# Seven half-size products for the gate and value matrices of the last layer

## The chip, the cores and the metric
One core of one Trainium2 chip runs the whole program as one launch. The metric is the device time of an execution in microseconds (us); the kernel before has a median of 1442.25 us over three runs (1439.95 to 1443.89). Engines: TensorE (PE, its weight loads PEld), VectorE (DVE), ScalarE (ACT), GpSimd (POOL) and SyncE (SP), which issues the transfers.

## The reference
Three layers follow each other. The last one is what the change touches:

```python
def reference(**kwargs):
    attn_out = _attn_ref(**attn_kwargs)             # B=2, H=8, S=768, D=64
    x = attn_out.transpose(0, 2, 1, 3).reshape(B * S, H * D)      # 1536 x 512
    x = _moe_ref(x=x, **moe_kwargs)                 # 8 experts, 512 -> 1024 -> 512, every token in each
    return _moe2_ref(x=x, **moe2_kwargs)

def _moe2_ref(x, w_gate, w_val, w_out):             # 512 -> 1536 -> 512
    gate = 1.0 / (1.0 + np.exp(-(x @ w_gate)))
    val = x @ w_val
    return (gate * val @ w_out).astype(np.float32)
```

## The kernel before
Every large matrix product is made of three matmuls: each operand is split into a rounded part (`h`, made on ACT) and a remainder (`l`, made on POOL or DVE as the difference), and h*h, h*l and l*h are added up in PSUM (`product`, L365 to L373). Tokens stand transposed in SBUF as `xh`, `xl` (features on partitions, 4 blocks of 128 features by 1536 tokens), the result of a layer as `acc` (12 tiles of 128 tokens by 512).

The feed-forward layers run in visits. A visit takes 256 hidden features. Experts 1 to 7 have 28 visits of the kind "fast". Each goes through the two batches of 768 tokens one after the other (`pair`), and treats the product of a 512x256 weight block with 768 tokens as a 2x2 product of operand blocks: seven products of blocks with half the features, half the hidden columns and 384 tokens, in place of eight. The seven left operands are sums and differences of weight blocks (`sum_steps` on POOL, then `form_step`, which splits each on ACT and POOL), the seven right operands are token blocks or sums of token blocks (`th`, `tl`, and the block (0,1) of `xh`, `xl`, which is overwritten by a sum). Results are added across four PSUM accumulators: `copied` keeps a partial sum in SBUF (ACT), `summed` adds one back (DVE), `hidden` rounds the hidden block (ACT) and appends its remainder to the list `late` (DVE). A product whose accumulator already holds a partial sum may start only when `copied` or `summed` has read it. PSUM banks: two for x, one each for y and z, and a ring of four (Y).

Between the products stand the second products (`unit_second`): for 128 tokens, six matmuls of 512 columns with the hidden blocks of the half visited before, then one DVE accumulation into `acc`. `slots` is called after each product and each second product; there the next visit's sums and forms and other side work are issued. What is written first in the program is issued first on its engine; the schedule is this order alone (`manual_schedule`), and every engine works through its queue in order.

After the last expert visit (`last`, which issues no forms of a next visit) the kernel before changes buffers (`moe.close()`) and works in a plain form. `turn_y` (L1312 to L1324) transposes one block of 128 features of four token tiles on TensorE, copies it to `xh` on ACT and subtracts it to `xl` on DVE; four of these stand between the last six second products, eight in the first visit after. Each of the six "glu" visits (`unit_first`, kind glu) goes through three chunks of 512 tokens; for each of its two hidden blocks it makes the gate product (12 matmuls of 512 columns), a sigmoid on ACT, the value product, the product with the gate on DVE, its rounding on ACT and remainder on DVE; then come four second products of the chunk before. The weights of the six visits are read as pieces of 512 KB (gate, value, out) from a DRAM copy made earlier (`load_piece`) and split whole (`split_steps`).

Of the kernel before, what the change touches and what calls it, by code (L numbers as in the profile page):

```python
# [26 lines left out]
PACE = (8, 13)  # L27
# [39 lines left out]
def tile_global_local_attention__then__sinkhorn_moe__then__glu(  # L67
# [96 lines left out]
    for f in range(NFF):  # L164
        visits.append(dict(kind="glu", f=f, chunks=chunks, slot=1 - len(visits) % 2, load=True))
# [3 lines left out]
    G0 = len(visits) - NFF  # L169
    last = G0 - 1  # L170
    turns = []


# [37 lines left out]

    def second_steps(n):

        vis = visits[n]
        r = raw[vis["raw"]][:, 4 * FQ : 8 * FQ]
        yield from split_halves(r, wh[vis["slot"]][1], wl[vis["slot"]][1])

    def split_steps(n):

        vis, steps = visits[n], []  # L220
        for j, part in enumerate(glu_weights(vis)):
            i = 3 * vis["f"] + j
            steps += split_halves(piece(i), *part)
            steps.append(lambda i=i: load_piece(i + 4))
        return steps
# [17 lines left out]
    def glu_weights(vis):  # L243

        g, v = state["glu", vis["f"] % 2]
        return g, v, (wh[vis["slot"]][1], wl[vis["slot"]][1])

# [10 lines left out]
    def w1_blocks(n):  # L258
        r = raw[visits[n]["raw"]][:, 0 : 4 * FQ]
        r = r.rearrange("p (k f c) -> p f k c", k=KD, f=2)  # L260
        return {(i, j): r[:, i, 2 * j : 2 * j + 2, :] for i in range(2) for j in range(2)}
# [138 lines left out]
    def unit_first(n, c, tick):  # L400
        vis = visits[n]
        m = c[1] * P
        if vis["kind"] == "moe":
            at = next_hid()
            hh, hl = hid[at]
            for f in range(2):
                ps = state["A"].next()[:, :m]
                first((wh[vis["slot"]][0], wl[vis["slot"]][0]), c, f, ps)
                nc.scalar.activation(out=hh[:, f, :m], in_=ps, func=AF.Relu)
                nc.vector.scalar_tensor_tensor(  # L410
                    out=hl[:, f, :m], in0=ps, scalar=0.0, in1=hh[:, f, :m].bitcast(F32),
                    op0=ALU.max, op1=ALU.subtract,
                )
                tick()
        else:
            at = HID + state["glu_hid"]
            state["glu_hid"] = 1 - state["glu_hid"]
            hh, hl = hid[at]
            gate_w, val_w, _ = glu_weights(vis)
            for f in range(2):  # L420
                ps = state["A"].next()[:, :m]
                first(gate_w, c, f, ps)
                sg = state["sg"].next()[:, :m]
                nc.scalar.activation(out=sg, in_=ps, func=AF.Sigmoid)
                tick()
                ps = state["A"].next()[:, :m]
                first(val_w, c, f, ps)
                z = state["z"].next()[:, :m]
                nc.vector.tensor_tensor(out=z, in0=ps, in1=sg, op=ALU.mult)  # L429
                nc.scalar.activation(out=hh[:, f, :m], in_=z, func=AF.Copy)  # L430
                nc.vector.tensor_tensor(
                    out=hl[:, f, :m], in0=z, in1=hh[:, f, :m].bitcast(F32), op=ALU.subtract
                )
                tick()
        return [(n, c[0] + j, at, j) for j in range(c[1])]

    def unit_second(n, t, at, j):
# [4 lines left out]
        if vis["kind"] != "glu":  # L442
# [30 lines left out]
    def turn():  # L473
        if turns:
            turns.pop(0)[1]()

    def run_visit(n, tick, ahead, pace=None):
# [3 lines left out]
        at = 0 if visits[n]["kind"] == "moe" else 1  # L481
        per = chunks[0][1] + (4 if at else 2)
        pace = pace or PACE[at]
        ahead = Paced(ahead, per * (len(chunks) - at) * pace // 12)
        side = tick

        def tick():
            side()
            if u >= at:
                ahead.tick()  # L490

        for u, c in enumerate(chunks):
            while any(at == c for at, _ in turns):
                turn()
# [14 lines left out]
    def pair(n, b, slots):  # L509
# [3 lines left out]
        snap, pre = state["snap"], state["pre"]  # L513
        x, y, z = state["X"].next()[:, :C], state["P2"][:, :C], state["P5"][:, :C]
        t_hid, late = next_hid(), []
        pending, done = state["pending"], []

        def run(i, ps, rhs, start=True):
# [8 lines left out]
            )  # L527

# [6 lines left out]
        def rest():  # L535
            for step in late:
                step()
            late.clear()

        def seconds(count):  # L540
            for _ in range(count):
                if pending:
                    unit_second(*pending.pop(0))
                rest()
                slots(None)

        def hidden(at, f, src):
            hh, hl = hid[at]
            nc.scalar.activation(out=hh[:, f, :C], in_=src, func=AF.Relu)  # L549
            late.append(  # L550
                lambda: nc.vector.scalar_tensor_tensor(  # L551
                    out=hl[:, f, :C], in0=src, scalar=0.0, in1=hh[:, f, :C].bitcast(F32),
# [4 lines left out]
        def summed(at, f, ps, kept):  # L557
            p = pre.next()
            nc.vector.tensor_tensor(out=p, in0=ps, in1=kept, op=ALU.add)  # L559
            hidden(at, f, p)  # L560
# [6 lines left out]
        slots(0)  # L567
        run(1, z, trans(0))
        copied(1, z)
        slots(1)  # L570
# [798 lines left out]
```

## Time and profile before

| | us |
|---|---|
| median of three runs | 1442.25 |
| lowest, highest | 1439.95, 1443.89 |
| span of the profiled execution | 1437.5 |
| TensorE busy in it | 1419.4 |
| DVE, POOL, ACT busy | 864.8, 568.8, 504.7 |
| first product of the last expert visit starts at | 1091.3 |
| first product of the last layer starts at | 1132.4 |
| last matmul ends about | 1433.2 |

The profile is of one execution; the page gives its span, from the first to the last instruction, and no time beside it. Busy times are shares of that span. In a timeline each line is one instruction or several alike in a row: its start, how long it took, the engine, the source line, what it wrote and read, and in brackets how long its engine had been idle and who ended that. Matmuls overlap in the pipeline, so the distance between two starts, not the length of one, is what a matmul costs.

### The profile page before, as it was taken

The page shows a single profiled execution, that of the slowest core. Times are in us where ns is not written, and L with a number is a line of the kernel's source. Part 1 is how long each engine was busy: PE and PEld are TensorE (multiplying, and loading weights), DVE is VectorE, ACT ScalarE, POOL GpSimd, SP SyncE. Part 2 cuts the span into 40 slices and gives each one's busy share as a digit, 9 for nine tenths or more (in the row PEclk, how much of TensorE's full clock was granted, in tenths as well). Part 3 has the DMA queues.
Part 4 walks back from the last instruction along what each step waited for, and adds up shares of the span by engine and source line. Part 5 has one row for each costly group of instructions (what it writes and reads, how often), then busy time and mean ns, then how long its engine had stood idle before and what let it go on. Part 6 is the DMA issues. An engine that isn't in the chain of part 4 may idle for free.

```text
span 1437.5 us, 19809 instructions
## 1 busy us (share of the span) xinstructions
PE 1419.4 (99%) x7286; PEld 1225.3 (85%) x7287; DVE 864.8 (60%) x1655; ACT 504.7 (35%) x1152; POOL 568.8 (40%) x618
## 2 busy tenths in 40 slices
PE   8999999999999999999999999999999999999998
PEld 4666888999999999999999899999999888888887
DVE  6676476677667666767676666666665533333333
ACT  5777222433333333333333333333333322122111
POOL 4554454554345454354454444445432221112110
PEclk9999999999999999999999999999999999999999
DMA  7751011132121222221213212213210110010002
GB/s 182 162 143 46 16 45 59 45 103 73 52 74 52 73 86 69 73 74 52 74 52 103 74 55 71 73 52 103 74 38 30 44 45 15 30 44 30 0 1 88
DMA packets 99192, 92.60 MB, mean 64 GB/s; under 512 B 55312, under 2 KB 73744, under 8 KB 99088
## 3 DMA queue, kind: packets, MB, share of 16 engines
q1 hardware_dynamic: 98800, 91.26, 20.5%
q8 instruction: 59, 0.97, 0.3%
q14 instruction: 45, 0.37, 0.1%
q10 hardware_dynamic: 288, 0.00, 0.0%
HBM read 78.66 MB, written 12.58 MB: 63 GB/s over the span
## 4 chain that ended last, share of the span: by engine, by line
PE 94%; DVE 2%; ACT 1%; POOL 1%; issue 1%; DMA 0%; SPq 0%; DVEq 0%; ACTq 0%; POOLq 0%
PE bank L371 30%; PE bank L373 30%; PE bank L372 30%; PE bank L870 1%; PE bank L922 1%; PE bank L908 1%; PE bank L844 1%; ACT e L884 0%; POOL wl L205 0%; DVE e L878 0%; PE bank L1317 0%; POOL e L896 0%; DMA lens<-in_n_local_dram 0%; SPq L649 0%; DVE hl L410 0%
## 5 line engine op out<-in xcount | busy, mean ns | idle before, releaser
L454 DVE SCALAR_TENSOR_TENSOR acc<-bank,gate,acc 128x512 f32<-128x512 f32 x336 | 251.6, 749 | 226.7 <-PE bank L373 220.9
L371 PE MATMUL bank<-wh,hh 128*128 128x512 f32 x912 | 359.3, 394 | 0.0
L373 PE MATMUL bank<-wh,hl 128*128 128x512 f32 x912 | 357.6, 392 | 0.0
L205 POOL TENSOR_TENSOR wl<-raw,wh 128x512 fp32r<-128x512 f32 (+1 forms) x196 | 209.4, 1085 | 372.4 <-ACT wh L204 367.9
L372 PE MATMUL bank<-wl,hh 128*128 128x512 f32 x912 | 356.1, 390 | 0.0
L371 PE MATMUL bank<-xh,wh 128*128 128x384 f32 (+1 forms) x720 | 252.2, 350 | 1.1 <-ACT aT L909 1.1
L372 PE MATMUL bank<-xl,wh 128*128 128x384 f32 (+1 forms) x720 | 249.8, 347 | 0.0
L373 PE MATMUL bank<-xh,wl 128*128 128x384 f32 (+1 forms) x720 | 249.8, 347 | 0.0
L373 PEld LDWEIGHTS bank<-wh,hl 128*128 128x128 f32 x912 | 171.3, 188 | 37.8
L549 ACT ACTIVATE hh<-kept 128x384 fp32r<-128x384 f32 x168 | 88.2, 525 | 310.6 <-DVE kept L559 310.6
L371 PEld LDWEIGHTS bank<-wh,hh 128*128 128x128 f32 x912 | 171.5, 188 | 26.1 <-issue 1.4
L372 PEld LDWEIGHTS bank<-wl,hh 128*128 128x128 f32 x912 | 171.7, 188 | 25.1
L371 PEld LDWEIGHTS bank<-xh,wh 128*128 128x128 f32 x720 | 135.3, 188 | 15.0 <-ACT aT L909 1.3
L372 PEld LDWEIGHTS bank<-xl,wh 128*128 128x128 f32 x720 | 135.5, 188 | 13.7 <-DVE xl L1322 0.5
L373 PEld LDWEIGHTS bank<-xh,wl 128*128 128x128 f32 x720 | 135.4, 188 | 6.3
L205 POOL TENSOR_TENSOR wl<-work,wh 128x256 fp32r<-128x256 f32 x112 | 94.1, 842 | 97.7 <-ACT wh L204 97.6
L563 ACT ACTIVATE kept<-bank 128x384 f32<-128x384 f32 x168 | 82.4, 491 | 119.7 <-PE bank L373 119.5
L551 DVE SCALAR_TENSOR_TENSOR hl<-kept,hh 128x384 fp32r<-128x384 f32 x168 | 113.8, 677 | 1.4 <-ACT hh L549 1.3
L373 PE MATMUL bank<-th,wl 128*128 128x384 f32 x336 | 113.0, 336 | 0.0
L371 PE MATMUL bank<-th,wh 128*128 128x384 f32 x336 | 112.9, 336 | 0.0
L372 PE MATMUL bank<-tl,wh 128*128 128x384 f32 x336 | 112.8, 336 | 0.0
L429 DVE TENSOR_TENSOR z<-bank,sg 128x512 f32<-128x512 f32 x36 | 24.9, 692 | 138.3 <-PE bank L373 138.3
(143 smaller groups left out, 1858.2 us busy)
## 6 DMA issues: line engine op xcount, KB each, us to landing
raw<-in_moe_w_dram SPq DMA_DIRECT2D x72, 512.0 KB, 4.2
glw<-work SPq DMA_DIRECT2D x36, 256.0 KB, 2.3
raw<-glw SPq DMA_DIRECT2D x18, 512.0 KB, 3.3
work<-in_moe_w_gate_dram SPq DMA_DIRECT2D x12, 512.0 KB, 3.9
work<-in_moe_w_val_dram SPq DMA_DIRECT2D x12, 512.0 KB, 3.9
work<-in_moe_w_out_dram SPq DMA_DIRECT2D x12, 512.0 KB, 3.9
qr<-in_q_dram SPq DMA_DIRECT2D x32, 96.0 KB, 2.7
kr<-in_k_dram SPq DMA_DIRECT2D x32, 96.0 KB, 2.9
```

The costliest lines, as they stand in the source:

```text
L205: nc.gpsimd.tensor_tensor(out=lo, in0=r, in1=h.bitcast(F32), op=ALU.subtract)
L371: nc.tensor.matmul(lhsT=ah, rhs=bh, start=first, stop=False, **mm)
L372: nc.tensor.matmul(lhsT=ah, rhs=bl, start=False, stop=False, **mm)
L373: nc.tensor.matmul(lhsT=al, rhs=bh, start=False, stop=end, **mm)
L429: nc.vector.tensor_tensor(out=z, in0=ps, in1=sg, op=ALU.mult)
L454: nc.vector.scalar_tensor_tensor(out=a, in0=ps, scalar=gate[:, t, e : e + 1], in1=a, op0=ALU.mult, op1=ALU.add,)
L549: nc.scalar.activation(out=hh[:, f, :C], in_=src, func=AF.Relu)
L551: lambda: nc.vector.scalar_tensor_tensor(out=hl[:, f, :C], in0=src, scalar=0.0, in1=hh[:, f, :C].bitcast(F32), op0=ALU.max, op1=ALU.subtract,)
L563: nc.scalar.activation(out=snap[:, i], in_=ps, func=AF.Copy)
L844: nc.tensor.transpose(ps[:, j * P : (j + 1) * P], raw_[u % QKB][:, j, :], ident)
L870: nc.tensor.matmul(out=ps[j][:, lo:KW], lhsT=qT[rows, own], rhs=kT[rows, keys], start=True, stop=True,)
L908: nc.tensor.transpose(ps[:, j, a, :], e[:, j, a * P : (a + 1) * P], ident)
```

## The change
The six visits become twelve of the kind "gate" and "val" in turn, and go through `pair` and `run_fast` like the experts, in the experts' buffers (`moe.close()` and all buffers made behind it go; `sg`, room for the eight sigmoid blocks of a visit, comes in their place). A gate visit writes sigmoids only; the value visit multiplies them in. `then` places three second products in each half of a visit, after products 1, 2 and 4. The token operands are made anew by `turned`, eight steps per batch: those of batch 0 are issued after products 4, 5 and 6 of the last expert visit's second half and between its last six second products, those of batch 1 after products 1 to 6 of the first gate visit's first half (the last three steps after product 6). The last expert visit's second products of batch 0 are moved to stand after products 1, 2 and 3, two each. The results leave from `acc`.

```diff
     for f in range(NFF):
-        visits.append(dict(kind="glu", f=f, chunks=chunks, slot=1 - len(visits) % 2, load=True))
+        slot = 1 - visits[-1]["slot"]
+        visits.append(dict(kind="gate", f=f, piece=3 * f))
+        visits.append(dict(kind="val", f=f, piece=3 * f + 1, slot=slot))
...
         else:
-            o = state["o"].next()
-            nc.vector.tensor_tensor(out=o, in0=ps, in1=a, op=ALU.add)
-            nc.sync.dma_start(out=out[t * P : (t + 1) * P, :], in_=o)
+            nc.vector.tensor_tensor(out=a, in0=ps, in1=a, op=ALU.add)
+            nc.sync.dma_start(out=out[t * P : (t + 1) * P, :], in_=a)
...
+            for step in late:
+                step()
+            late.clear()
...
+        def then(i):
+            slots(i)
+            for _ in range(min(counts.get(i, 0), len(pending))):
+                unit_second(*pending.pop(0))
+                for step in late:
+                    step()
+                late.clear()
                 slots(None)
...
+            if kind == "gate":
+                nc.scalar.activation(out=state["sg"][b, half, f], in_=src, func=AF.Sigmoid)
+                return
...
+            if kind == "val":
+                z = pre.next()
+                nc.vector.tensor_tensor(out=z, in0=src, in1=state["sg"][b, half, f], op=ALU.mult)
+                nc.scalar.activation(out=hh, in_=z, func=AF.Copy)
+                late.append(
+                    lambda: nc.vector.tensor_tensor(
+                        out=hl, in0=z, in1=hh.bitcast(F32), op=ALU.subtract
+                    )
+                )
+                return
...
         def before(i):
             side()
-            if i is None and ahead:
+            if n == G0 and i is not None and i > 0:
+                trans_step(1, 3 if i == 6 else 1)
+            if ahead and (i is None or not expert):
                 ahead.pop(0)()
...
-            elif i > 0:
+                return
+            if i > 0 and more:
                 form_step(n + 1, i - 1)
+            if n == last and i > 3:
+                trans_step(0, 1)
+
+        all_ = {1: 1, 2: 1, 3: 1, 4: 1, 5: 2}
+        half = {1: 1, 2: 1, 4: 1}
+        pair(n, 0, before, all_ if expert else half)
...
+        pair(n, 1, after, {1: 2, 2: 2, 3: 2} if n == last else all_ if expert else half)
...
+                load_piece(vis["piece"] + 4)
+                if vis["kind"] == "val":
+                    load_piece(vis["piece"] + 5)
...
+        def turn(s, k, half):
+            kk = 2 * k + s
+            ps = state["Y"].next()[:, :C]
+            t0 = b * TB + half * TC
+            for j in range(TC):
+                nc.tensor.transpose(
+                    ps[:, j * P : (j + 1) * P], acc(t0 + j)[:, kk * P : (kk + 1) * P], ident
+                )
+            return ps
+
+        def whole(s, k, half, ps):
+            h, lo = tokens(k, s, b, half)
+            nc.scalar.activation(out=h, in_=ps, func=AF.Copy)
+            nc.vector.tensor_tensor(out=lo, in0=ps, in1=h.bitcast(F32), op=ALU.subtract)
+
+        def less(x, y):
+            t = temps.next()
+            nc.vector.tensor_tensor(out=t, in0=x, in1=y, op=ALU.subtract)
+            return t
+
+        def put(i, s, r):
+            th, tl = state["t"]
+            split_one(r, th[:, i, s, b, :], tl[:, i, s, b, :])
+
+        def r11(s):
+            live["r11", s] = ps = turn(s, 0, 0)
+            whole(s, 0, 0, ps)
+
+        def r12(s):
+            ps = turn(s, 0, 1)
+            live["r12", s] = r = temps.next()
+            nc.scalar.activation(out=r, in_=ps, func=AF.Copy)
+            live["t0", s] = t = less(r, live["r11", s])
+            put(0, s, t)
+
+        def r22(s):
+            ps = turn(s, 1, 1)
+            live["t1", s] = t = less(ps, live["t0", s])
+            put(1, s, t)
+            whole(s, 1, 1, ps)
+            r = live["r12", s]
+            nc.vector.tensor_tensor(out=r, in0=ps, in1=r, op=ALU.subtract)
+            put(2, s, r)
+
+        def r21(s):
+            ps = turn(s, 1, 0)
+            whole(s, 1, 0, ps)
+            split_one(less(ps, live["t1", s]), *tokens(0, s, b, 1))
+
+        return [lambda f=f, s=s: f(s) for f in (r11, r12, r22, r21) for s in range(2)]
...
+    for n in range(F0, len(visits)):
         if n == last:
             doubles.finish()
         run_fast(n, doubles.tick)
...
+        if n == last:
+            while state["pending"]:
+                unit_second(*state["pending"].pop(0))
+                trans_step(0, 1)
+            trans_step(0, 8)
     flush(no_tick)
```

## Rows read from the trace of the kernel before

**Rows 1.** The page: each engine's busy time, share of the span, instructions.
```profile
PE 1419.4 (99%) x7286; PEld 1225.3 (85%) x7287; DVE 864.8 (60%) x1655; ACT 504.7 (35%) x1152; POOL 568.8 (40%) x618
```

**Rows 2.** Windows: stretch, length, each engine's busy time and count, granted clock, DMA.
```profile
1106.83:1433.20 326.37, 326.34 (x1459) 268.82 (x1458) 119.12 (x175) 73.35 (x128) 46.37 (x36) 1.00 0.09 31
1230.00:1280.00 50.00, 50.00 (x219) 41.00 (x219) 16.82 (x25) 10.51 (x18) 7.70 (x6) 1.00 0.10 34
```

**Rows 3.** Timeline of TensorE: product 1, a unit, product 2 of the last expert visit.
```profile
1107.87 0.34 PE L371 MATMUL bank<-th,wh 128*128 128x384 f32 x1
...
1108.91 0.39 PE L371 MATMUL bank<-wh,hh 128*128 128x512 f32 x1
...
1110.28 0.34 PE L371 MATMUL bank<-th,wh 128*128 128x384 f32 x1
```

**Rows 4.** Timeline of TensorE: four transposes between second products, end of the expert layer.
```profile
1123.73 0.60 PE L1317 MATMUL bank<-ident,acc 128*128 128x128 f32 x4
1124.08 0.48 PE L371 MATMUL bank<-wh,hh 128*128 128x512 f32 x1
1124.40 0.39 PE L372 MATMUL bank<-wl,hh 128*128 128x512 f32 x1
```

**Rows 5.** Timeline of DVE in the last expert visit.
```profile
1110.48 0.75 DVE L454 SCALAR_TENSOR_TENSOR acc<-bank,gate,acc 128x512 f32<-128x512 f32 x1 [2.31 <-PE bank L373]
...
1115.98 0.55 DVE L551 SCALAR_TENSOR_TENSOR hl<-kept,hh 128x384 fp32r<-128x384 f32 x1
1116.45 0.55 DVE L559 TENSOR_TENSOR kept<-bank,kept 128x384 f32<-128x384 f32 x1
...
1118.41 1.46 DVE L551 SCALAR_TENSOR_TENSOR hl<-kept,hh 128x384 fp32r<-128x384 f32 x1
```

**Rows 6.** Timeline of ACT: last expert visit, then two operations back to back.
```profile
1108.13 0.49 ACT L563 ACTIVATE kept<-bank 128x384 f32<-128x384 f32 x1 [0.55 <-PE bank L373]
...
1114.60 0.53 ACT L549 ACTIVATE hh<-kept 128x384 fp32r<-128x384 f32 x1 [2.53 <-DVE kept L559]
...
1135.45 0.60 ACT L424 ACTIVATE sg<-bank 128x512 f32<-128x512 f32 x1 [4.99 <-PE bank L373]
1135.94 0.59 ACT L1321 ACTIVATE xh<-bank 128x512 fp32r<-128x512 f32 x1
```

**Rows 7.** Timeline of POOL beside the remainder at 1118.41.
```profile
1118.15 1.29 POOL L205 TENSOR_TENSOR wl<-raw,wh 128x512 fp32r<-128x512 f32 x1 [24.28 <-ACT wh L204]
```

**Rows 8.** Groups by line over the run: busy us, mean ns of one.
```profile
L551 DVE SCALAR_TENSOR_TENSOR hl<-kept,hh 128x384 fp32r<-128x384 f32 x168 | 113.8, 677 | 1.4 <-ACT hh L549 1.3
L205 POOL TENSOR_TENSOR wl<-work,wh 128x256 fp32r<-128x256 f32 x112 | 94.1, 842 | 97.7 <-ACT wh L204 97.6
L204 ACT ACTIVATE wh<-work 128x256 fp32r<-128x256 f32 x112 | 45.0, 404 | 0.0
L205 POOL TENSOR_TENSOR tl<-work,th 128x768 fp32r<-128x768 f32 x6 | 11.8, 1971 | 6.4 <-ACT th L204 6.4
L205 POOL TENSOR_TENSOR wgl<-raw,wgh 128x512 fp32r<-128x512 f32 x6 | 7.8, 1298 | 91.0 <-ACT wgh L204 91.0
```

**Rows 9.** Timeline of DVE and ACT: one hidden block of the first glu visit.
```profile
1138.66 0.69 DVE L429 TENSOR_TENSOR z<-bank,sg 128x512 f32<-128x512 f32 x1 [1.40 <-PE bank L373]
...
1139.39 0.63 ACT L430 ACTIVATE hh<-z 128x512 fp32r<-128x512 f32 x1 [2.85 <-DVE z L429]
...
1140.05 0.69 DVE L431 TENSOR_TENSOR hl<-z,hh 128x512 fp32r<-128x512 f32 x1 [0.70 <-ACT hh L430]
```

**Rows 10.** TensorE's clock: timeline of the start, window behind the end.
```profile
1.18 4.65 PE L693 MATMUL bank<-zeros 128*128 128x512 bf16 x12 [1.18 <-DVE zeros L689]
...
7.37 1.03 PE L693 MATMUL bank<-zeros 128*128 128x512 bf16 x4
...
1437.00:1439.00 2.00, 0.00 (x0) 0.00 (x0) 0.00 (x0) 0.00 (x0) 0.00 (x0) 0.91 0.01 4
```

**Rows 11.** DMA issues of the weight pieces: count, KB each, us to landing.
```profile
raw<-glw SPq DMA_DIRECT2D x18, 512.0 KB, 3.3
```

More of the change, by code (lines that the diff above doesn't have):

```diff
@@ L26 @@
 HID = 3
-PACE = (8, 13)
+PACE = 8
 LAG = 3
@@ L168, in tile_global_local_attention__then__sinkhorn_moe__then__glu @@
     F0 = NB0 + NQ
-    G0 = len(visits) - NFF
+    G0 = len(visits) - 2 * NFF
     last = G0 - 1
-    turns = []
     queues = [[], []]
@@ L402, in unit_first @@
         m = c[1] * P
[L403 to L434, printed above, removed]
+        at = next_hid()
+        hh, hl = hid[at]
+        for f in range(2):
+            ps = state["A"].next()[:, :m]
+            first((wh[vis["slot"]][0], wl[vis["slot"]][0]), c, f, ps)
+            nc.scalar.activation(out=hh[:, f, :m], in_=ps, func=AF.Relu)
+            nc.vector.scalar_tensor_tensor(
+                out=hl[:, f, :m], in0=ps, scalar=0.0, in1=hh[:, f, :m].bitcast(F32),
+                op0=ALU.max, op1=ALU.subtract,
+            )
+            tick()
         return [(n, c[0] + j, at, j) for j in range(c[1])]
@@ L471, in flush @@
             tick()
-    def turn():
-        if turns:
-            turns.pop(0)[1]()
     def run_visit(n, tick, ahead, pace=None):
         chunks = visits[n]["chunks"]
[L481 to L484, printed above, removed]
+        ahead = Paced(ahead, (chunks[0][1] + 2) * len(chunks) * (pace or PACE) // 12)
         side = tick
@@ L488, in tick @@
             side()
[L489 to L494, printed above, removed]
+            ahead.tick()
+        for c in chunks:
             pending = unit_first(n, c, tick)
@@ L533, in block, with hidden @@
             return lambda s: tokens(k, s, b, half)
[L535 to L544, printed above, removed]
-                slots(None)
-        def hidden(at, f, src):
-            hh, hl = hid[at]
-            nc.scalar.activation(out=hh[:, f, :C], in_=src, func=AF.Relu)
+        def then(i):
[5 more added lines that the diff above has]
+                late.clear()
+                slots(None)
+        def hidden(half, f, src):
+            if kind == "gate":
+                nc.scalar.activation(out=state["sg"][b, half, f], in_=src, func=AF.Sigmoid)
+                return
+            if half not in at:
+                at[half] = next_hid()
+            hh, hl = (x[:, f, :C] for x in hid[at[half]])
+            if kind == "val":
[8 more added lines that the diff above has]
+                return
+            nc.scalar.activation(out=hh, in_=src, func=AF.Relu)
             late.append(
                 lambda: nc.vector.scalar_tensor_tensor(
-                    out=hl[:, f, :C], in0=src, scalar=0.0, in1=hh[:, f, :C].bitcast(F32),
+                    out=hl, in0=src, scalar=0.0, in1=hh.bitcast(F32),
                     op0=ALU.max, op1=ALU.subtract,
@@ L555, in hidden, with summed @@
             )
-        def summed(at, f, ps, kept):
+        def summed(half, f, ps, kept):
             p = pre.next()
             nc.vector.tensor_tensor(out=p, in0=ps, in1=kept, op=ALU.add)
-            hidden(at, f, p)
+            hidden(half, f, p)
         def copied(i, ps):
@@ L623, in run_fast @@
+        half = {1: 1, 2: 1, 4: 1}
+        pair(n, 0, before, all_ if expert else half)
         for step in ahead:
             step()
-        pair(n, 1, after)
-        if fast:
+        pair(n, 1, after, {1: 2, 2: 2, 3: 2} if n == last else all_ if expert else half)
+        for step in seconds:
+            step()
+        if more:
             form_step(n + 1, 6)
-            load(visits[n + 1]["raw"])
+            vis = visits[n + 1]
+            if "piece" not in vis:
+                load(vis["raw"])
+            else:
+                load_piece(vis["piece"] + 4)
+                if vis["kind"] == "val":
+                    load_piece(vis["piece"] + 5)
@@ L631, in tile_global_local_attention__then__sinkhorn_moe__then__glu, with trans_step @@
+    def trans_step(b, count):
+        if ("turned", b) not in state:
+            state["turned", b] = turned(b)
+        for step in state["turned", b][:count]:
+            step()
+        del state["turned", b][:count]
     with tc.tile_pool(name="attn", bufs=1) as ap:
```

145 lines of the change are left out of this document (52 added, 93 removed).

## The prediction

> **What bounds it now.** I read the page's busy shares first: TensorE is busy 99% of the 1437.5 us [rows 1]. From the start of the second half of the last expert visit (1106.83) to the end of the matmuls (1433.20), a window of 326.37 us, it is busy 326.34 [rows 2]: the stretch that the change rewrites has no hole to close, its clock is granted at 1.00, and time falls only by less matmul work. The other engines idle more than half of it (DVE 119, ACT 73, POOL 46 us), so on averages they could take more. Averages do not decide here: each is an in-order queue, so I walk the queues.
>
> **TensorE's own work.** Dense steps: 50 us hold 219 matmuls of 512 columns, 0.228 us each [rows 2]. A half-size product (six matmuls of 384) lasts 1108.91-1107.87 = 1.04 us; a token tile's second product ("unit", six of 512) 1110.28-1108.91 = 1.37 [rows 3]. Four transposes push the next matmul 0.35 us back and lengthen that one from 0.23 to 0.32, so 0.11 each, 0.34 for three [rows 4]. Removed: 6 x 144 = 864 matmuls of 512 columns, 197 us. Added: 12 visits x 2 halves x 7 products, 168 x 1.04 = 175 us. The 72 units stay, the 48 transposes go from twelve fours to sixteen threes. From 1106.83 on: 7 products 7.3, 12 expert units 16.5, transposes 5.5, 168 products 174.7, 72 units (1.374) 98.9: 302.6 us, dense, against 326.4: **-23.8 us**. Nothing in that depends on waits; everything below does.
>
> **Durations for the walk.** A product's end reaches ACT and DVE 0.26 us after the next one's start at 1107.87, a unit's 0.20 after 1110.28 [rows 3, 5, 6]; from DVE to ACT and back 0.03 to 0.04 pass [rows 9]. 128x384: DVE 0.55; ACT 0.49 from PSUM, 0.53 from SBUF, and 0.40 for a 256-wide form [rows 5 to 8]. POOL is 0.84 for 256, 1.3 for 512, 1.97 for 768; 384 is not there, bounds 0.84 and 1.3, I take 1.0 [rows 8]. Back to back, ACT starts 0.11 and DVE 0.08 before the last one's end [rows 5, 6]. The same numbers on an expert visit (two halves of 7 products and 6 units, 31.0 us) give no wait, as in the trace, where the window is full.
>
> **Turning batch 0 (end of the last expert visit).** Before, four 4-transposes stood between units, each followed by one ACT copy and one DVE subtraction [rows 4]. Now eight steps of three transposes, each with up to three ACT, three DVE and two POOL operations that need each other in turn. Count from the end of the last product. ACT still has five operations queued (a Relu, a form, a copy, a Relu, a form) and copies r12 of slice 0 only at 2.65-3.14; DVE subtracts until 3.73; that read frees the bank which r12 of slice 1 is to be transposed into: start 3.76 instead of 1.78, **2.0 lost**. Unit 2 needs the bank of r11, slice 1, read by the next such subtraction (ends 5.56): **1.5**. r22 is subtract 0.55, ACT put and copy 0.95, DVE two more 1.0, and holds its bank through all; its second slice reuses one of five scratch tiles and so waits for POOL's 1.0 us remainder of the first. The transposes of r21, slice 1, wait **2.2** for it; behind them waits of 0.3, 0.3, 0.6 (the first batch-1 transposes need the last expert update) and 0.3. Sum **7.2 us**. Bounds: 0 if the order of the queues hid all; 9 with POOL at 1.3.
>
> **Turning batch 1 (first gate visit, first half).** No units are pending there: 7 products and 8 transposes, 10 us of TensorE. ACT gets 3 copies, 4 sigmoids, 16 operations of the turn and 2 roundings of w_out: 10 us back to back, but each subtraction between two of them leaves ACT idle 1.1 us. Count from the first gate product: TensorE has finished the half and its transposes at 10.8 and products 0 and 1 of the second half at 12.9. Product 2 adds into the bank that copy 0 of this half must have read, and copy 0 is queued on ACT behind the whole turn, three steps of which are issued after product 6. ACT: sigmoid of product 6 done at 14.4; r22 slice 1 (0.55, 0.95, 1.0, 0.5; it too waits for POOL) to 17.8; r21 of each slice (copy 0.49, DVE twice 1.0, ACT 0.53) to 19.8 and 21.8; copy 0 to 22.2. **9.3 us lost.** Bounds: 4.7 if half the rounds overlap, 11 with POOL at 1.3.
>
> **Steady visits.** A value half asks per hidden block, on DVE, for sum, gate product, wait for ACT's rounding, remainder. The trace of before has the same round at 512 columns: 1138.66 to 1140.74 [rows 9]. At 384: 0.55+0.04+0.55+0.03+0.53+0.03+0.55 = 2.3 us; the remainder stands in DVE's queue ahead of the next block's sum. Products 3 to 6 end at 0, 1.04, 3.45 and 4.49 (a unit stands between 4 and 5); rounds start at 0.26, 2.5, 4.7, 6.95 (one accumulation, 0.69, between). The last rounding ends at 8.05, two forms of the next matrix follow on ACT, copy 0 ends at 9.0; TensorE wants its bank at 7.95. **1.05 lost** at each gate's start, 0.46 (no forms ahead) between a value visit's halves: five times 1.5. The first value visit, with no pending units in its first half, loses 1.0+0.9. Sum **9.4 us**. Bounds: 0 (rounds 10% shorter fit) and 14.
>
> **SBUF against POOL.** The remainder that started at 1118.41 took 1.46 us: POOL held 1118.15 to 1119.44, and 1119.44+0.43 is its end [rows 5, 7]. On average such a remainder takes 0.68 [rows 8] where it takes 0.55 with POOL idle and an addition from PSUM 0.55 always [rows 5]. The Trainium skill, SBUF — State Buffer, "Who interferes with whom", says that a DVE instruction with two SBUF inputs and a POOL instruction that reads SBUF exclude each other for a whole instruction; that row agrees. This speaks against the change: gate products and remainders (up to 7 per value half) have two SBUF inputs, while POOL's forms double. With every overlap paid in full the walk loses 3.3 us more, with the mean excess of before (0.1 to 0.13 of 0.55) about half: I take **1.5**, bounds 0 and 3.3.
>
> **Clock.** No wait of 9 us exists before. After the matmuls end at 1433.2, the granted clock of 1437 to 1439 is 0.91, so it fell in there; at the start twelve 512-column matmuls take 4.65 us, most of them at the 1.2 GHz level, while four at 7.4 us come 0.21 apart, the 2.4 GHz level [rows 10]. Twelve at the later pace would take 2.7 us, so regaining the clock cost 1.9. I take **1.9** once, bounds 0 and 4.
>
> **At nothing.** Weight loads stay 18 x 512 KB, 3.3 us each [rows 11], issued on SP a visit (20 us) ahead of their sums; if a landing were late, sums, forms and product 0 would slip with it. POOL's 8 sums, 14 forms and 2 w_out remainders per f (20 us of 47) hide beside products; uncovered they would cost a form, 0.8 us, each. The sigmoid's function table costs nothing new: a sigmoid and a copy stand back to back on ACT before, without a load between [rows 6]. The tail keeps one DVE addition and one transfer; the transfer leaves from the accumulator, no buffer to wait for.
>
> **Sum.** -23.8+7.2+9.3+9.4+1.5+1.9 = +5.5 us. On the profiled execution, 1437.5 span to 1443. The page gives no time of it beside the span; the shown median is 4.8 above the span, and I keep that distance: 1442.25+5.5 = **1447.8 us**. So seven eighths of the products and no gain: holes eat it.
>
> **Rivals.** (0.3%, about 4.3 us, is what a measurement can tell from no change.)
> - *Forecast*, 1447.8, own range 1444.5 to 1451: 0.35.
> - *The clock does not fall* in the long wait: 1445.9. For it: no wait in this trace is so long, so none shows a fall inside the run; against: the end of the run [rows 10]. 0.15.
> - *The exclusion is paid in full* (the SBUF page's rule): +1.8, 1449.6. 0.12.
> - *The long wait is half* (ACT finds its copy early): 1443. 0.12.
> - *Value rounds stay hidden*, the other side: the four rounds with copy 0 take under 7.9 us instead of 9.0. Then 7.5 of the steady loss and the 1.5 vanish: -3.5, 1438.8. For it: 10% decides; DVE is busy under 40% [rows 2]. Against: rounds are sums of measured durations. 0.15.
> - *Both last ones*: -8 to -12, 1430 to 1434, faster. 0.05.
> - *Longer turns and a second fall of the clock*: 1455 and more. 0.06.
> That fewer products are not really issued can be excluded: the loop is 7 x 6 matmuls.
>
> Over 1446.6 lie two thirds of the forecast (0.23), 0.06, 0.10, 0.06 and 0.02: slower 0.47. Under 1437.9: 0.06+0.05, faster 0.11. The rest, 0.42, is within. Range 1437 to 1454.
>
> **What will show it.** TensorE columns: 384-wide matmuls 0.173 apart throughout, dense part 23 to 24 us shorter: wrong if not. Transposes of batch 0 with about 7 us of TensorE idle whose releasers are DVE; product 2 of the first gate visit's second half with 9 us, released by ACT's copy; after it a granted clock under 1 for some microseconds. Then 1.0 and 0.5 us at product 2, every 47 us, released by ACT. Visits of about 23.3 (gate) and 23.8 (value). The prediction is wrong if the gate and value visits run without holes (1439 or less), or if the first gate visit's ACT queue is through before TensorE needs its copy.

## The result, and the profile after

The changed kernel takes **1450.11 us** (median of 4 runs, 1448.97 to 1451.56); the kernel before, timed beside it, 1442.01 (4 runs, 1439.95 to 1443.89). The ratio is **1.0062, 95% interval 1.0048 to 1.0076**: 8.1 us slower by the medians, where +5.5 was forecast. The interval is 6.9 to 11.0 us, so the forecast of the change lies under it. The profiled execution took 1449.29 us, with a span of 1447.5. That span is 10.0 us over the one of before, more than the medians differ: a kernel's executions spread over some 3 us, so where terms are compared, waits within one trace are counted, and where kernels are compared, medians.

The page answers [rows 1] (each engine's busy time, share of the span, instructions): TensorE has more instructions, less busy time, and 97% of the span where it had 99%.

```profile
PE 1405.5 (97%) x7430; PEld 1239.7 (86%) x7431; DVE 910.6 (63%) x1767; ACT 561.7 (39%) x1328; POOL 650.4 (45%) x742
```

Windows of after, as in [rows 2] (stretch, length, busy time and count of each engine, granted clock, DMA). The first runs from the same matmul as the window of before, the start of the second half of the last expert visit, to the end of the matmuls. It is 335.90 us against 326.37: the whole loss is in it, bar 0.7 us that lie ahead of it. The second holds the steady visits. The other two are the stretches where the clock was granted at half, its 1.2 GHz level.

```profile
1107.49:1443.39 335.90, 312.26 (x1603) 283.60 (x1602) 164.19 (x287) 130.26 (x304) 125.98 (x156) 0.98 0.09 30
1186.00:1437.00 251.00, 243.62 (x1264) 223.75 (x1263) 123.91 (x217) 95.93 (x224) 90.51 (x116) 1.00 0.08 27
...
1128.87:1132.28 3.41, 2.88 (x7) 2.19 (x8) 0.48 (x1) 0.52 (x1) 1.92 (x3) 0.50 0.44 137
1159.59:1169.83 10.24, 5.61 (x18) 5.61 (x19) 2.60 (x5) 4.53 (x12) 4.46 (x5) 0.50 0.01 2
```

Now the waits, one place at a time. **Turning batch 0**, timeline of TensorE (start, duration, line and operation, idle time before and what released it):

```profile
1125.14 0.40 PE L361 MATMUL bank<-wh,hl 128*128 128x512 f32 x1
1127.52 0.55 PE L622 MATMUL bank<-ident,acc 128*128 128x128 f32 x3 [1.98 <-DVE work L634]
1129.40 0.79 PE L359 MATMUL bank<-wh,hh 128*128 128x512 f32 x1 [1.34 <-DVE work L634]
1129.99 0.63 PE L360 MATMUL bank<-wl,hh 128*128 128x512 f32 x1
...
1137.55 0.39 PE L361 MATMUL bank<-wh,hl 128*128 128x512 f32 x1
1139.86 0.55 PE L622 MATMUL bank<-ident,acc 128*128 128x128 f32 x3 [1.92 <-DVE work L658]
```

Three long waits, all released by DVE's subtractions of the turn, as the walk had them. A wait's price is the step from one matmul to the next less the same step without a wait (0.173 us for 384 columns, 0.229 for 512, 0.109 from one transpose to the next, 0.03 from the last transpose to the matmul behind it): 2.15 at 1125.14, 1.58 before 1129.40, 2.08 at 1137.55. With five small ones (0.36, 0.36, 0.34, 0.19 and 0.16, the last three already in the first gate visit) that is 7.2 us.

**Turning batch 1**, TensorE, then ACT beside it. Product 2 of the first gate visit's second half starts 9.50 us after the matmul before it, 9.33 too late, and its releaser is copy 0 of the first half (L534):

```profile
1154.72 0.34 PE L361 MATMUL bank<-th,wl 128*128 128x384 f32 x1
1164.22 0.69 PE L359 MATMUL bank<-th,wh 128*128 128x384 f32 x1 [9.16 <-ACT kept L534]
1164.70 0.52 PE L360 MATMUL bank<-tl,wh 128*128 128x384 f32 x1
1165.02 0.52 PE L361 MATMUL bank<-th,wl 128*128 128x384 f32 x1
```

```profile
1157.73 0.47 ACT L629 ACTIVATE xh<-bank 128x384 fp32r<-128x384 f32 x1
1159.29 0.52 ACT L203 ACTIVATE th<-work 128x384 fp32r<-128x384 f32 x1 [1.09 <-DVE work L658]
1159.72 0.47 ACT L629 ACTIVATE xh<-bank 128x384 fp32r<-128x384 f32 x1
1161.28 0.52 ACT L203 ACTIVATE xh<-work 128x384 fp32r<-128x384 f32 x1 [1.09 <-DVE work L634]
...
1163.26 0.52 ACT L203 ACTIVATE xh<-work 128x384 fp32r<-128x384 f32 x1 [1.08 <-DVE work L634]
1163.69 0.85 ACT L534 ACTIVATE kept<-bank 128x384 f32<-128x384 f32 x2
```

Read the rhythm: every 2 us ACT rounds, stands 1.1 us while DVE subtracts, rounds again. ACT is not busy, it is in a ping-pong, and copy 0, for which TensorE stands, is last in its queue.

**A steady value round**, DVE, then ACT, POOL and TensorE, to be held against [rows 9]: sum (L530), gate product (L512), the wait for ACT's rounding (L513), remainder (L515). The rows of 1195 to 1197 are the end of another such round, at one of the four gate starts that are alike.

```profile
1236.14 0.56 DVE L530 TENSOR_TENSOR kept<-bank,kept 128x384 f32<-128x384 f32 x1 [0.42 <-PE bank L361]
1236.73 0.56 DVE L512 TENSOR_TENSOR kept<-kept,work 128x384 f32<-128x384 f32 x1
1237.88 0.56 DVE L515 TENSOR_TENSOR hl<-kept,hh 128x384 fp32r<-128x384 f32 x1 [0.59 <-ACT hh L513]
1238.36 0.55 DVE L530 TENSOR_TENSOR kept<-bank,kept 128x384 f32<-128x384 f32 x1
1238.94 0.56 DVE L512 TENSOR_TENSOR kept<-kept,work 128x384 f32<-128x384 f32 x1
...
1241.15 0.56 DVE L512 TENSOR_TENSOR kept<-kept,sg 128x384 f32<-128x384 f32 x1
1242.67 0.56 DVE L515 TENSOR_TENSOR hl<-kept,hh 128x384 fp32r<-128x384 f32 x1 [0.96 <-ACT hh L513]
```

```profile
1195.92 0.52 ACT L513 ACTIVATE hh<-kept 128x384 fp32r<-128x384 f32 x1 [0.84 <-DVE kept L512]
...
1196.97 0.85 ACT L534 ACTIVATE kept<-bank 128x384 f32<-128x384 f32 x2
...
1237.32 0.53 ACT L513 ACTIVATE hh<-kept 128x384 fp32r<-128x384 f32 x1 [2.81 <-DVE kept L512]
...
1242.12 0.53 ACT L513 ACTIVATE hh<-kept 128x384 fp32r<-128x384 f32 x1 [1.75 <-DVE kept L512]
...
1244.84 0.85 ACT L534 ACTIVATE kept<-bank 128x384 f32<-128x384 f32 x2
```

```profile
1238.23 0.81 POOL L204 TENSOR_TENSOR wl<-work,wh 128x256 fp32r<-128x256 f32 x1 [2.90 <-ACT wh L203]
```

```profile
1196.01 0.39 PE L361 MATMUL bank<-wh,hl 128*128 128x512 f32 x1
1197.49 0.44 PE L359 MATMUL bank<-th,wh 128*128 128x384 f32 x1 [1.09 <-ACT kept L534]
...
1243.59 0.39 PE L361 MATMUL bank<-wh,hl 128*128 128x512 f32 x1
1245.36 0.45 PE L359 MATMUL bank<-th,wh 128*128 128x384 f32 x1 [1.38 <-ACT kept L534]
```

DVE idles half a microsecond or more in each round while the next block's sum stands behind the remainder. The gate's product 2 starts 1.54 too late at 1245.36 and 1.25 at the other four gate starts (1197.49 is one); between a value visit's halves it is 0.49 five times, and the first value visit pays 1.00 and 0.76: 10.8 us.

### The profile page after: what moved, and what is told of

Read it like the earlier page. It is cut to its first block, busy times and chain, and to the rows that moved or that the text cites. A ratio compares the mean times of both kernels' runs of the same rounds, so it can differ in the third digit from the quotient of the medians.

```text
span 1447.5 us, 20637 instructions
## 1 busy us (share of the span) xinstructions
PE 1405.5 (97%) x7430; PEld 1239.7 (86%) x7431; DVE 910.6 (63%) x1767; ACT 561.7 (39%) x1328; POOL 650.4 (45%) x742
## 4 chain that ended last, share of the span: by engine, by line
PE 89%; DVE 5%; ACT 3%; issue 1%; POOL 1%; DMA 0%; SPq 0%; DVEq 0%; ACTq 0%; POOLq 0%
PE bank L359 29%; PE bank L361 28%; PE bank L360 28%; PE bank L915 1%; PE bank L967 1%; PE bank L953 1%; DVE kept L512 1%; ACT e L929 1%; DVE kept L530 1%; PE bank L889 1%; DVE hl L515 0%; ACT wh L203 0%; POOL wl L204 0%; DVE e L923 0%; ACT kept L534 0%
## 5 line engine op out<-in xcount | busy, mean ns | idle before, releaser
L204 POOL TENSOR_TENSOR wl<-raw,wh 128x512 fp32r<-128x512 f32 (+1 forms) x220 | 221.4, 1020 | 341.3 <-ACT wh L203 330.5
L359 PE MATMUL bank<-xh,wh 128*128 128x384 f32 x768 | 260.0, 338 | 2.0 <-ACT aT L954 1.1
L360 PE MATMUL bank<-xl,wh 128*128 128x384 f32 x768 | 258.2, 336 | 0.0
L361 PE MATMUL bank<-xh,wl 128*128 128x384 f32 x768 | 257.9, 336 | 0.0
L204 POOL TENSOR_TENSOR wl<-work,wh 128x256 fp32r<-128x256 f32 x160 | 129.0, 807 | 176.8 <-ACT wh L203 176.2
L359 PE MATMUL bank<-th,wh 128*128 128x384 f32 x480 | 163.5, 341 | 17.1 <-ACT kept L534 17.1
L534 ACT ACTIVATE kept<-bank 128x384 f32<-128x384 f32 x240 | 115.8, 489 | 160.1 <-PE bank L361 160.0
L361 PE MATMUL bank<-th,wl 128*128 128x384 f32 x480 | 161.9, 337 | 0.0
L360 PE MATMUL bank<-tl,wh 128*128 128x384 f32 x480 | 161.8, 337 | 0.0
L530 DVE TENSOR_TENSOR kept<-bank,kept 128x384 f32<-128x384 f32 x240 | 132.3, 551 | 42.4 <-PE bank L361 41.8
L359 PEld LDWEIGHTS bank<-xh,wh 128*128 128x128 f32 x768 | 144.5, 188 | 12.6 <-ACT aT L954 1.3
```

The costliest lines, as they stand in the source:

```text
L204: nc.gpsimd.tensor_tensor(out=lo, in0=r, in1=h.bitcast(F32), op=ALU.subtract)
L359: nc.tensor.matmul(lhsT=ah, rhs=bh, start=first, stop=False, **mm)
L360: nc.tensor.matmul(lhsT=ah, rhs=bl, start=False, stop=False, **mm)
L361: nc.tensor.matmul(lhsT=al, rhs=bh, start=False, stop=end, **mm)
L534: nc.scalar.activation(out=snap[:, i], in_=ps, func=AF.Copy)
```

## The experiments

Each ratio is to the kernel before, timed beside it: 1440.74 us (19 runs) beside the first four, 1440.84 (9 runs) beside the others. "After" in the diffs is the changed kernel.

**Is it the order on DVE?** The rival is that rounds are simply too long. The remainder of a value block is issued behind the next block's sum and gate product instead of ahead of them; same instructions, same counts.

```diff
...
-    for step in late:
-        step()
-    late.clear()
+    if kind != "val":
+        for step in late:
+            step()
+        late.clear()
...
     nc.scalar.activation(out=hh, in_=z, func=AF.Copy)
+    for step in late:
+        step()
+    late.clear()
     late.append(
...
```

> In a value visit the remainder of a hidden block is issued on DVE behind the next block's sum and gate product instead of ahead of them; no instruction is added or taken away. Theory (order of the in-order queues): DVE no longer waits for ACT's rounding between two blocks, copy 0 of the next half is read in time, and the waits of 1.25 and 0.49 us at product 2 of every visit (1.0 and 0.75 in the first) go: 5 x 1.74 + 1.75 = 10.4 us less than the changed kernel, about 1440. Rival (load: DVE, ACT and POOL have more to do than TensorE's shorter time hides, or hold each other up at SBUF): the same work in another order gains nothing, 1449 to 1451.

Measured: 1439.0 us (10 runs), ratio 0.9987 (0.9978 to 0.9997), 11.1 under after's median. Of twelve steady waits one of 0.40 is left, at 1238.79, in front of this row of TensorE:

```profile
1239.42 0.45 PE L359 MATMUL bank<-th,wh 128*128 128x384 f32 x1 [0.24 <-ACT kept L538]
```

So all but 0.4 of the 10.8 us was order, not work. The trace holds a second thing. DVE and POOL (the remainder is L519 in this kernel):

```profile
1233.00 0.56 DVE L513 TENSOR_TENSOR kept<-kept,work 128x384 f32<-128x384 f32 x1
1233.47 1.13 DVE L519 TENSOR_TENSOR hl<-kept,hh 128x384 fp32r<-128x384 f32 x1
...
1235.12 0.54 DVE L519 TENSOR_TENSOR hl<-kept,hh 128x384 fp32r<-128x384 f32 x1
```

```profile
1233.44 0.75 POOL L204 TENSOR_TENSOR wl<-work,wh 128x256 fp32r<-128x256 f32 x1 [2.90 <-ACT wh L203]
1234.50 0.75 POOL L204 TENSOR_TENSOR wl<-work,wh 128x256 fp32r<-128x256 f32 x1 [0.31 <-ACT wh L203]
```

The remainder that starts with 0.72 us of a POOL instruction left takes 1.13; the one that starts with 0.13 left takes 0.54. An operation with one input in PSUM shows nothing of the kind: in after, the sum at 1249.20 starts with 1.27 us of a POOL instruction left and takes 0.56.

**Is the long wait ACT's queue?** The last two steps of batch 1's turn move behind products 0 and 1 of the second half, so copy 0 stands ahead of them.

```diff
-                trans_step(1, 3 if i == 6 else 1)
+                trans_step(1, 1)
...
+            if n == G0 and i < 2:
+                trans_step(1, 1)
             if i > 0 and more:
                 form_step(n + 1, i - 1)
```

> The last two of the eight steps that turn batch 1 are issued after products 0 and 1 of the first gate visit's second half instead of after product 6 of its first half. Theory (order): copy 0 stands behind six steps instead of eight on ACT, so the single wait of 9.3 us becomes one of about 5.3 and two of 1.4 and 1.6: 1 us less by the waits alone, and 0 to 2.6 us more because a shorter wait may leave the clock up: 1446.5 to 1449. It stays a small gain because the rounds between ACT and DVE last as long as before. Rival (load): no change, 1450.

Measured: 1447.88 (4 runs), ratio 1.0054 (1.0037 to 1.0071), against 1.0062 for after. The wait is cut as expected, and what is late next takes part of it back: 5.33, then 0.43 and 0.74 us (I had expected 1.4 and 1.6) instead of 9.33, the last two before products 3 and 4.

```profile
1159.47 0.69 PE L359 MATMUL bank<-th,wh 128*128 128x384 f32 x1 [5.17 <-ACT kept L534]
...
1164.52 0.69 PE L359 MATMUL bank<-th,wh 128*128 128x384 f32 x1 [0.39 <-ACT kept L534]
```

The queue holds the wait. But 2.8 us less wait gave 1.2 us by the ratios, whose intervals are wider than that. The trace shows where some of it went: the clock is low behind the wait for 10.24 us in both kernels, and the shorter wait leaves 25 matmuls in that stretch instead of 18, 1.0 us more at 0.15 each. In the profiled execution the clock was also low for 6.83 us at the first turn where after has 3.41, most of which the third wait there gives back (1.04 instead of 2.08).

**What does the clock cost?** Matmuls whose result nobody reads fill the waits of both turns: 7, 5 and 7 in batch 0's, 36 in the long one.

```diff
+def idle_fill(count):
+    w = wh[visits[last]["slot"]][1]
+    for _ in range(count):
+        nc.tensor.matmul(out=state["P2"], lhsT=w[:, 0:P], rhs=w[:, 0:512], start=True, stop=True)
...
+        if n == G0 and b == 1:
+            idle_fill(36)
         run(2, x, trans(1), start=False)
```

> Matmuls of 512 columns that nothing reads are put into the long waits: 7, 5 and 7 where batch 0 is turned, 36 ahead of product 2 in the first gate visit's second half; they fit into the waits. Theory (clock): the two falls to 1.2 GHz in the profile (3.4 and 10.2 us long) do not come, and the matmuls that ran at 0.43 and 0.32 us return to 0.23 and 0.17: 1.5 + 2.6 = 4.1 us less, 1446; the waits themselves keep their ends. Rival (the slow clock only stretched work that would have waited for DVE and ACT anyway): 1449 to 1451.

Measured: 1445.71 (5 runs), ratio 1.0037 (1.0023 to 1.0051). Window of the two turns, then TensorE in the long wait:

```profile
1123.00:1180.00 57.00, 53.49 (x278) 45.71 (x276) 28.39 (x54) 28.82 (x67) 32.11 (x36) 1.00 0.08 28
```

```profile
1152.80 0.34 PE L361 MATMUL bank<-th,wl 128*128 128x384 f32 x1
1152.98 8.33 PE L468 MATMUL bank<-wh 128*128 128x512 f32 x36
1162.35 0.45 PE L359 MATMUL bank<-th,wh 128*128 128x384 f32 x1 [1.04 <-ACT kept L541]
```

Product 2 starts 9.55 us after the last useful matmul, as in after (9.50), but the clock is granted in full and the steps behind it are 0.17 apart, not 0.32. The ratios differ by 0.0025, 3.6 us, and their intervals just touch; the longer steps in after's trace add up to 3.9 us. So two falls of the clock cost about that.

**Are the turns round trips or work?** Each step of a turn takes both slices side by side, so that DVE subtracts for one while ACT rounds for the other; two more scratch tiles; batch 0's steps behind products 4 and 6 and two units, batch 1's behind products 1, 2, 4 and 6.

```diff
-            if n == G0 and i is not None and i > 0:
-                trans_step(1, 3 if i == 6 else 1)
+            if n == G0 and i in (1, 2, 4, 6):
+                trans_step(1, 1)
...
-def r12(s):
-    ps = turn(s, 0, 1)
-    ...
+def r12():
+    pss = [turn(s, 0, 1) for s in range(2)]
+    live["r12"] = rs = [temps.next() for s in range(2)]
+    for r, ps in zip(rs, pss):
+        nc.scalar.activation(out=r, in_=ps, func=AF.Copy)
+    live["t0"] = ts = [less(r, ps) for r, ps in zip(rs, live["r11"])]
+    for s, t in enumerate(ts):
+        put(0, s, t)
...
-state["temps"] = Ring(work[:, i * C : (i + 1) * C] for i in range(5))
+state["temps"] = Ring([*(work[:, i * C : (i + 1) * C] for i in range(5)), sg[:, 4], sg[:, 5]])
```

> The two slices of each turning step go side by side: both transposes, then the operations of both on ACT, then both on DVE, so that one engine works on a slice while the other has its neighbour; seven scratch tiles instead of five. Number and size of the operations are the same. Theory (rounds between ACT and DVE): the waits of the turning, 7.5 us for batch 0 and 9.3 for batch 1, shrink to about 3.5 and 2; the clock stays up (4 us): 15 us less, 1435, of which the larger ring alone makes 2. Rival (load): ACT, DVE and POOL have the same busy time to get through, gain under 3 us (the ring and part of the clock), 1447 or more.

Measured: 1437.5 (9 runs), ratio 0.9979 (0.9969 to 0.9989), 12.6 under after's median. Turning waits 3.35, 0.35 and 2.70 instead of 7.2 and 9.33; the steady ones as in after. One fall of the clock is left (window 1153.30 to 1156.71, 0.50), behind the 2.70:

```profile
1127.58 0.50 PE L359 MATMUL bank<-wh,hh 128*128 128x512 f32 x1 [3.11 <-DVE work L634]
```

```profile
1152.65 0.45 PE L359 MATMUL bank<-th,wh 128*128 128x384 f32 x1 [2.53 <-ACT kept L534]
```

2.5 us over what I expected: I had counted on 3.5 us of waits at batch 0 and 2 at batch 1, where 3.7 and 2.7 came, and on a clock that stays up. The wait of 3.35 ends with the first slice's subtraction (1126.97 to 1127.52). DVE had stood 0.86 us for ACT's copies (from 1126.40), and these came in ACT's queue behind two roundings of hidden blocks and two forms, a row that starts at 1124.99. The edit also issues some steps earlier, so one run does not separate that from the pairing. The trace shows what pairing does to a step: the last one, r21, takes ACT from 1150.07 to 1152.13 for both slices, 2.06 us, where after needs 3.97 for the two in turn (1159.72 to 1163.69).

**Both together**, batch 0's steps one product later (5 and 6).

```diff
-    if n == last and i in (4, 6):
+    if n == last and i in (5, 6):
```

> Slices side by side with seven scratch tiles, and the value remainder behind the next block's sum, together; the first two turning steps of batch 0 after products 5 and 6. Theory (order): both gains add up, since they lie in different visits: of the changed kernel's 29 us of waits about 6 stay (2.5 to 3 in each turning, 0.4 once), 1450 - 11 - 13 = 1426; TensorE's shorter work then shows, 15 us or 1% under the kernel before. Rival (a common limit in ACT, DVE or POOL shows up once one of them is mended): less than the sum, 1432 or more.

Measured: **1425.96** (4 runs), ratio 0.9897 (0.9881 to 0.9914). Three waits are left, 2.51, 0.35 and 2.70, and one fall of the clock. Windows of the fall and of everything behind it:

```profile
1152.14:1155.56 3.42, 3.42 (x13) 3.42 (x12) 0.56 (x1) 0.94 (x3) 3.42 (x5) 0.50 0.02 5
1155.56:1417.00 261.44, 261.44 (x1367) 242.33 (x1366) 137.31 (x234) 103.41 (x243) 98.47 (x126) 1.00 0.10 36
```

TensorE's waits are gone from the steady visits: the same products that made the kernel slower make it faster once the queues are ordered for them.

**Does the form of the instruction decide on contention?** In after no gate product and no remainder of a value block is lengthened, while the expert visits' remainders, another form (scalar_tensor_tensor), are. So: the value blocks' two operations in that form too, with a scalar of 1.

```diff
-nc.vector.tensor_tensor(out=z, in0=src, in1=state["sg"][b, half, f], op=ALU.mult)
+nc.vector.scalar_tensor_tensor(out=z, in0=src, scalar=1.0, in1=state["sg"][b, half, f], op0=ALU.mult, op1=ALU.mult)
...
-nc.vector.tensor_tensor(out=hl, in0=z, in1=hh.bitcast(F32), op=ALU.subtract)
+nc.vector.scalar_tensor_tensor(out=hl, in0=z, scalar=1.0, in1=hh.bitcast(F32), op0=ALU.mult, op1=ALU.subtract)
```

> Of the value visits' 96 DVE operations per run with two SBUF inputs that were tensor_tensor, all (gate product and remainder) become scalar_tensor_tensor with a factor of 1. In the changed kernel none of them was longer than 0.56 us, though POOL was running when 11 of the gate products with two SBUF inputs started. Theory (the hold-up depends on the form of the instruction): in the new form those that start while POOL runs take 0.6 to 1.1 us, as the experts' remainders do, and the time rises by 1 to 4 us. Rival (two SBUF inputs alone decide, and the few cases happened to miss POOL's reads): durations and time as in the changed kernel.

Measured: 1448.35, one run. My theory fell: the form changes nothing. Groups of this kernel (busy us, mean ns):

```profile
L518 DVE SCALAR_TENSOR_TENSOR hl<-kept,hh 128x384 fp32r<-128x384 f32 x48 | 26.8, 558 | 23.0 <-ACT hh L516 23.0
```

and of after:

```profile
L515 DVE TENSOR_TENSOR hl<-kept,hh 128x384 fp32r<-128x384 f32 x48 | 26.8, 558 | 23.0 <-ACT hh L513 23.0
```

With the reordered kernel's tensor_tensor of 1.13 us this leaves the rival: two SBUF inputs beside a POOL instruction are enough, in either form, and in after the two all but miss each other: no value block's operation of this kind starts with more than 0.14 us of POOL's left.

**The fill on the best order.** Eight unread matmuls in each of the two long waits that are left.

```diff
+        if n == G0 and b == 1:
+            idle_fill(8)
         run(2, x, trans(1), start=False)
...
     pss = [turn(s, 0, 1) for s in range(2)]
+    if b == 0:
+        idle_fill(8)
```

> The same as the kernel with both, and 8 unread matmuls of 512 columns in each of its two waits of 2 to 3 us. Theory (clock): the one fall of the clock for 3.4 us that the kernel with slices side by side showed does not come: 0.5 to 1.5 us less than the kernel with both. Rival: the fill only takes up the wait, same time within 0.1%.

Measured: **1424.71** (4 runs), ratio 0.9884 (0.9868 to 0.9901), the fastest version; its median is 1.25 under the one without the fill, but the intervals overlap, and 1.25 us is within the 0.1% of the rival too, so the time does not decide between the two. The trace shows the fall gone: the two turns at 1.00, then the steady visits.

```profile
1122.00:1160.00 38.00, 36.74 (x208) 32.90 (x207) 23.89 (x46) 26.00 (x62) 27.66 (x31) 1.00 0.04 15
1160.00:1418.00 258.00, 258.00 (x1347) 238.84 (x1346) 136.49 (x233) 100.30 (x235) 96.20 (x123) 1.00 0.11 37
```

**The scratch ring alone.** Seven scratch tiles instead of five, nothing else.

```diff
-state["temps"] = Ring(work[:, i * C : (i + 1) * C] for i in range(5))
+state["temps"] = Ring([*(work[:, i * C : (i + 1) * C] for i in range(5)), sg[:, 4], sg[:, 5]])
```

> The changed kernel with seven scratch tiles for the turning instead of five, and nothing else. Theory: each second slice's subtraction no longer waits for POOL's remainder of the first: 1 us less for batch 0, 0.9 for batch 1, 1448; the rest of the gain of the slices side by side (10 to 11 us) is their order. Rival (the scratch tiles were the cause of the turning's waits): 1440 or less.

Measured: 1446.27 (6 runs), ratio 1.0035 (1.0023 to 1.0048). The wait of 2.08 at r21 of slice 1 is now 0.96, the long one 8.42:

```profile
1139.73 0.55 PE L622 MATMUL bank<-ident,acc 128*128 128x128 f32 x3 [0.80 <-DVE work L658]
```

```profile
1163.17 0.69 PE L359 MATMUL bank<-th,wh 128*128 128x384 f32 x1 [8.26 <-ACT kept L534]
```

So POOL's remainder of the slice before held a tile, and with it both turns, for 2.0 us together. The rest of the 3.9 us between the two ratios is within their intervals. Nine tenths of the long wait have nothing to do with the tiles.

## Why the prediction was right, step by step

The direction and the mechanism were right: the dense gain came in full, and holes ate it. The holes were sized 29.3 us together and measured 33.3. The single terms were off by more than that: 5.5 us were missing in the steady visits (1.4), the clock (2.0) and the longer steps behind waits (2.1, for which there was no term), and 1.5 for SBUF never came. That the time came within 2.3 us of the forecast is in part luck.

- **Dense work, -23.8.** The window of 335.90 us less waits of 27.3 (7.2, 9.3, 10.8) and 3.9 for the clock is 304.7. A matmul behind a wait has a longer step to the next, 0.28 instead of 0.17 behind 1245.36; some 20 of those are 2 us. That leaves 302.7, where 302.6 was forecast (its printed terms add up to 302.9, a slip of 0.3): the gain is the 23.8, and the holes are 33.3.
- **Turning batch 0, +7.2.** Measured 7.2; the three long ones 2.15, 1.58 and 2.08 against 2.0, 1.5 and 2.2. POOL's 384 columns, taken at 1.0 between bounds of 0.84 and 1.3, lasted 0.99 to 1.02.
- **Turning batch 1, +9.3.** Measured 9.33, at the matmul named and behind the copy named. Moving two steps out of the way of the copy cut it to 5.33; pairing the slices, with r22 issued one and two products earlier, to 2.70.
- **Steady visits, +9.4.** Measured 10.8; the mechanism is shown by the new order, which takes away all but 0.4. The size was 15% short. The walk of the rounds was right: counted from the end of product 3 (1188.29 in the round that ends at 1197.49) they start at 0.27, 2.49, 4.70 and 6.99, where 0.26, 2.5, 4.7 and 6.95 were forecast. Behind the last one small delays add up: its rounding ends at 8.16 instead of 8.05, copy 0 (the first of the pair at 1196.97, 0.47 long) at 9.14 instead of 9.0, and TensorE starts 0.05 behind the copy, where the walk had nothing. So 1.05 became 1.25 at four gate starts. At the fifth it is 1.54: there the third block's rounding comes 0.41 us behind its gate product (DVE 1241.15 + 0.56 to ACT 1242.12), 0.12 in the other visits. I give that delay no cause: no run was made for it. The same 0.41 stands in the reordered kernel at 1237.13, ahead of the one wait that is left there.
- **SBUF against POOL, +1.5.** Measured 0, the one term that failed outright. I priced it with a mean excess of the expert visits, whose remainders meet POOL in the middle (690 ns a piece in after too). In a value round POOL's form starts behind ACT's form, which stands behind the very rounding that DVE's remainder waits for, so the two meet only at their ends: the remainder of 1237.88 has 0.21 us to go when POOL begins at 1238.23, and takes its 0.56; the gate product at 1238.94 starts with 0.10 us of that POOL instruction left and takes 0.56. The Trainium skill, SBUF — State Buffer, "Who interferes with whom", says that a DVE instruction with two SBUF inputs contends with a POOL instruction that reads SBUF. The trace does not refute that: where the new order lets them meet, 0.72 us of POOL gave 1.13 us, the rest of POOL's instruction plus 0.41. With at most 0.14 left the same sum is 0.55, no more than the operation takes alone. What a meeting costs depends on where the two fall in time, and I took an average from a place with another phase. In the reordered kernel the 48 remainders average 643 ns instead of 558, 4 us of DVE time; the best order has them too (1.12 and 0.86 us) and no wait of TensorE in the steady visits.
- **Clock, +1.9.** Measured 3.9: behind 1129.40 one step of 0.59 and five of 0.43 cost 1.3 us, behind 1164.22 one of 0.48 and sixteen of 0.32 cost 2.6; and the kernel with filled waits is 3.6 us faster. The step that failed is "I take 1.9 once": it fell twice, I had looked for it behind the wait of 9 us alone, and there too it cost more. The Trainium skill, TensorE: Matmul & The Clock Gate, "What's actually happening", says that the clock goes back to its lower level when TensorE has been idle. By that the long wait was the candidate, and the trace agrees (10.24 us at 0.50). The fall behind two waits of 2.15 and 1.58 I had not counted.
- **At nothing.** Held: transfers of weight pieces land in 3.6 us instead of 3.3 [rows 11]; none of TensorE's waits in the window is put down to a transfer or to POOL.
- **Where the time stands.** By the trace's terms: -23.8 + 7.2 + 9.3 + 10.8 + 3.9 + 2.1 for the longer steps behind the waits is +9.5, with 0.7 upstream about the +10.0 of the spans. The medians say +8.1.

Of the rivals, "the clock does not fall", "the long wait is half" and "value rounds stay hidden" are each refuted by rows above. "The exclusion is paid in full" gave 1449.6, the figure nearest to the measured one, and is refuted all the same: that term measured 0. "A second fall of the clock" came, though without the longer turns that I had tied to it.

## What to carry to other kernels

Work that needs several engines in turn is priced by its round trips in the in-order queues, not by busy shares: with TensorE at 97% and ACT at 39%, two changes of order, with two more scratch tiles, were worth 24 us, as much as the matmuls saved. So when a cheaper algorithm shortens TensorE's steps, first walk each queue over one period with the new lengths, and issue the second half of a round trip behind the next one's first half; side by side where two slices do the same. Price contention from the phase in which two instructions will meet, and look for a fall of the clock behind every wait, not only the longest: here one came behind waits of 2.15 and 1.58 us.

## What the runs showed of the hardware that was not expected

- The granted clock fell to 0.50 behind waits of 2.15 and 1.58 us (after, the reordered kernel and the one with seven tiles 3.41 us long, with two steps moved 6.83), and stayed whole behind the same two waits in the profile with the other instruction form (1123 to 1145 at 1.00): with the same code there it came in one execution and not in another. Behind 2.70 us it fell for 3.41 in both profiles with that wait; behind the long wait, 5.33 to 9.33, for 10.24 in every profile without the fill. The length of a wait alone does not tell: at the first turn of the paired kernel nothing fell behind a wait of 3.35 us, nor behind 2.51 with both orders. Unread matmuls in the waits kept the clock whole.
- A DVE instruction with two SBUF inputs that starts beside a POOL instruction lasts the rest of that one plus 0.41 to 0.42 us (0.72 to 1.13; in the best order without the fill 0.44 to 0.86), and nothing is seen of rests up to 0.14 us. With one input in PSUM it takes its 0.56 beside 1.27 us of POOL.
